# A recurrent-memory attention kernel with a gated unit: score matmuls set between projection matmuls, in place of a V stage with ten tile buffers and transposing DMAs

## The chip, the cores and the metric

The kernel runs on one core of a Trainium2 chip. The metric is device time in microseconds of one execution. The kernel before has a median of 1620.66 us over four runs (1619.23 to 1621.8). The profile below comes from one more execution, which took 1622.41 us; its span, from the first to the last instruction, is 1620.70 us, and the remaining 1.7 us lie around it.

## The reference, cut to what matters

A layer norm feeds two branches whose product is added to x:

```python
def _A_ref(x, mem0, Wq, Wk, Wv, Wo, seg_len):      # 32 heads of 128, segments of 32, memory of 8
    ...
    for s in range(n_seg):
        h = jnp.concatenate([mem, xs], axis=1)      # 8 memory + 32 token rows
        q, k, v = ...                               # h @ Wq, h @ Wk, h @ Wv
        p = _softmax(jnp.where(mask[None, None], scores, -1e9), axis=-1)
        o = jnp.einsum('bhte,hed->btd', jnp.einsum('bhqk,bhke->bhqe', p, v), Wo)
        mem = o[:, :M, :].copy()                    # memory of the next segment
        outs.append(o[:, M:, :])
def _B_ref(x, w_gate, w_up, w_down):
    h = _sigmoid(x @ w_gate) * (x @ w_up)
    return h @ w_down
x = A_x; xn = _layernorm(x)
return x + _A_ref(xn, ...) * _silu(_B_ref(xn, ...))
```

There are 2048 tokens of 1024 features, hence 64 segments, and the gated unit has 3584 hidden features.

## The kernel before, in words

The loop over segments is not run one by one. Memory rows are estimated in advance from sums of V over each segment, all segments then go through attention together, and a check at the end raises a flag if the estimate was not good enough (a sequential version stands behind that flag). Tokens are held as 16 tiles of 128; xnT is the normalized input with features on partitions, 8 chunks of 128 (KC = 8).

**The V stage** (lines 274 to 480) computes V for all tokens. Its unit is a pair (g, t): column group g of 1024 (of 4) for token tile t (of 16), in two halves of 512 columns (`v_half`, L354): eight matmuls each (L361) into a PSUM buffer of `psb` (four buffers, tag "big"), which ACT copies to the tile v_sb (L363). `v_store` (L365) sends v_sb to vp_dram from SP's queue; `seg_sums` (L375) adds up segments on DVE; `gather_sums` (L379) moves the sums in 16 small copies; `wo_part` (L402) multiplies them by a piece of Wo on TensorE. `normalize` (L311) makes one tile of the normalized input, and `transpose_x` (L327) turns it by eight PE transposes (L330) and an ACT copy (L332). `pack` (L340) copies xnT into xq, where memory rows are interleaved. Weights come by `load_wv` (L288) and `wo_load` (L397).

The order is a list written by hand, `units` (L424): tiles 0 to 7 for group 0, then for group 1, then tiles 8 to 15, each for group 0 and group 1, then groups 2 and 3. Tiles 8 to 15 are not turned on TensorE. `store_xn` (L334) writes them to xn_dram and `turn_xn` (L337) reads them back with a transposing DMA, both on SP's queue. V tiles come from `vs2`, ten buffers on the right side of the memory, until `begin_glu` (L254) closes that pool at unit 57 and opens the gate pools in its place; the last units use `vsp`, three buffers. Every half is copied by ACT. Within this stage TensorE, SP, ACT and DVE follow program order.

**Between V and the heads** (L481 to L541) the memory estimates are worked out, with steps of the gate and up matmuls (`glu_gate_up_steps`, L145; `filler`, L261) filling TensorE.

**The heads stage** (L544 to L672) runs 32 heads in a pipeline of one head's length. While head h is projected (`proj_steps`, L578: q and k, five blocks each, eight matmuls of 424 columns per block, L589, and an ACT copy at its end, L591), head h-1 does its attention (`attn_steps`, L641). Its scores come in five batches (`s_batch`, L594): matmuls of 99 columns (L603), one for the first segment (L605), then Exp on ACT (L607) and a mask on DVE (L609). P times V comes in seven groups of three matmuls and a single one (`pv_batch`, L613; L628, L623), each followed by a reciprocal and a product on DVE (L631, L632). A plan by hand sets which of them stand after which of the ten projection blocks:

```python
plan = [[("s", 0), ("s", 1)], [("s", 2)], [("s", 3)], [("s", 4), ("v", 0)], [("v", 1)], [("v", 2), ("v", 3)],
        [("v", 4)], [("v", 5), ("v", 6)], [("v", 7)], []]
```

So scores run back to back, nine at first and four or five afterwards, and PV three or six at a time. Here TensorE and SP follow program order. In the last turn of the loop no head is projected, and `filler` steps stand between the plan's steps.

**After the heads** the rest of the gate and up matmuls, then the down projection (L763), the output projection (L773) and the combination. The change touches none of that.

Of the kernel before, what the change touches and what calls it, by code (L numbers as in the profile page):

```python
# [19 lines left out]
P = 128  # L20
# [183 lines left out]
def kernel(ctx, tc, A_x, A_mem0, A_Wq, A_Wk, A_Wv, A_Wo, A_seg_len, B_x, B_w_gate, B_w_up, B_w_down, out,  # L204
# [34 lines left out]
    xn_dram = tc.dram_tile([S // 2, DM], BF16, name="xn_dram")  # L239
# [10 lines left out]
    es_r = ExitStack()  # L250
    vs2 = es_r.enter_context(tc.tile_pool(name="vs2", bufs=10, side="right"))
    glus = []

    def begin_glu():  # L254
        es_r.close()
        gu_w = es_x.enter_context(tc.tile_pool(name="gu_w", bufs=2, side="right", reuse_waits="tile"))
        gu_sb = es_x.enter_context(tc.tile_pool(name="gu_sb", bufs=2, side="right", reuse_waits="tile"))
        glus.append(glu_gate_up_steps(nc, gu_w, gu_sb, xnT, B_w_gate, B_w_up, hT_dram, psb, "big", 4))
        filler(1)

    def filler(n=1):  # L261
        for _ in range(n):
            next(glus[0], None)
# [10 lines left out]
    with ExitStack() as es:  # L274
# [31 lines left out]
        svqa = hwp.tile([P, 2, NT, 1024 // SEG], F32, name="svqa", tag="w")  # L306
        svqs = [svqa[:, 0], svqa[:, 1], svq, svq]
# [26 lines left out]
        def store_xn(t):  # L334
            nc.sync.dma_start(xn_dram[(t - NT // 2) * P:(t - NT // 2 + 1) * P, :], xns[t][:])

        def turn_xn(t):  # L337
            nc.sync.dma_start_transpose(xnT[:, :, t * P:(t + 1) * P], xn_dram[(t - NT // 2) * P:(t - NT // 2 + 1) * P, :])

# [14 lines left out]
        def v_half(g, t, j):  # L354
            if j == 0:
                v_sbs[g, t] = (vsp if glus else vs2).tile([P, 1024], BF16, name="v_sb")
            v_sb = v_sbs[g, t]
            cg = 2 * g + j
            v_ps = psb.tile([P, 512], F32, name="v_ps", tag="big")
            for c in range(KC):  # L360
                nc.tensor.matmul(v_ps[:], lhsT=xnT[:, c, t * P:(t + 1) * P], rhs=wv_sb[:, c, cg * 512:(cg + 1) * 512],  # L361
                                 start=(c == 0), stop=(c == KC - 1))
            nc.scalar.copy(v_sb[:, j * 512:(j + 1) * 512], v_ps[:])  # L363

        def v_store(g, t):  # L365
            v_sb = v_sbs[g, t]
# [8 lines left out]
        def seg_sums(g, t):  # L375
            nc.vector.tensor_reduce(svqs[g][:, t, :], v_sbs[g, t][:].rearrange("p (b i) -> p b i", i=SEG), axis=AX.X, op=ALU.add,
                                    apply_transpose=True)

        def gather_sums(g):  # L379
            src = svqs[g][:, :, :].rearrange("p t (h b) -> p b h t", b=4)  # L380
# [42 lines left out]
        HT = NT // 2  # L423
        units = [(g, t) for g in range(2) for t in range(HT)]  # L424
        units += [(g, t) for t in range(HT, NT) for g in range(2)]
        units += [(g, t) for g in range(2, NG) for t in range(NT)]
        turns = {HT + 2 * i: HT + i for i in range(4)}
        turns.update({2 * HT + 2 * i: HT + 4 + i for i in range(4)})
        loads = {2 + i: (2 + i // 2, i % 2) for i in range(4)}
        loads.update({18 + 3 * i: (4 + i // 2, i % 2) for i in range(4)})  # L430
        loads.update({38 + 2 * i: (6 + i // 2, i % 2) for i in range(4)})
        wload = {n: hg for hg, n in enumerate((33, 35, 39, 42, 50, 54, 59, 61))}
        wpart = (38, 41, 44, 47, 55, 58)
        for n, (g, t) in enumerate(units):
            if n == 0:
                v_half(0, 0, 0)
                transpose_x(1)
                normalize(2)
                v_half(0, 1, 0)
                normalize(3)  # L440
                for c in range(KC):
                    nc.tensor.transpose(mt0[:, c, :], m0[:, c * P:(c + 1) * P], ident[0:M, 0:M])
                nc.vector.tensor_copy(cmT[:, :, NM:NCM], mt0[:])
                nc.vector.tensor_copy(xq[:, :, X0 + SEG:NP], mt0[:])
                nc.vector.tensor_copy(g1b[:, :, NM:NCM], mt0[:])
                transpose_x(2)
                v_half(0, 0, 1)
            elif n == 1:
                v_half(0, 1, 1)
            else:  # L450
                v_half(g, t, 0)
                v_half(g, t, 1)
            v_store(g, t)
            if 0 < n < HT - 3:
                normalize(n + 3)
            if 0 < n < HT - 2:
                transpose_x(n + 2)
            if n in turns:
                normalize(turns[n])
                store_xn(turns[n])  # L460
            if n - 2 in turns:
                turn_xn(turns[n - 2])
            if n > 0:
                seg_sums(*units[n - 1])
            if g == 1:
                pack(t)
            for k, q in ((2 * NT, 0), (2 * NT, 1), (3 * NT, 2)):
                if n == k:
                    o1 = gather_sums(q)
                    pend += [(2 * q, o1, 0), (2 * q + 1, o1, 4)]  # L470
            if n in loads:
                cg, i = loads[n]
                load_wv(cg, i * 4, i * 4 + 4, nc.scalar)
            if n == 57:
                begin_glu()
            if n in wload:
                wo_ts.append(wo_load(wload[n], nc.scalar))
            if n in wpart:
                hg, o1, h0 = pend.pop(0)
                wo_part(acc1, wo_ts.pop(0), hg, o1[:, h0:h0 + 4, :])  # L480
        es_v.close()  # L481
        wo_t = wo_ts
        seg_sums(*units[-1])
# [65 lines left out]
    with ExitStack() as es:  # L549
# [28 lines left out]
        def proj_steps(h):  # L578
# [5 lines left out]
            for (w_, dst) in ((wq, qt), (wk, kt)):  # L584
                for i in range(NBLK):
# [5 lines left out]
                    nc.scalar.copy(dst[:, a:b], pr[:, 0:b - a])  # L591
                    yield

        def s_batch(h, i):  # L594
# [6 lines left out]
            for j in range(n):  # L601
                o = (j0 + j) * TR
                nc.tensor.matmul(s_ps[:, j * TR:(j + 1) * TR], lhsT=kt[:, o:o + P], rhs=qt[:, o:o + TR], start=True, stop=True)  # L603
            if last:
# [5 lines left out]
            if last:  # L610
                nc.vector.tensor_tensor(pT[0:L, X0:NP], pT[0:L, X0:NP], mask0[:], op=ALU.mult)

        def pv_batch(h, i):  # L613
# [10 lines left out]
            else:  # L624
                R = TR
                for j in range(n):
                    o = (j0 + j) * TR
                    nc.tensor.matmul(o_ps[:, j, :], lhsT=pT[:, o:o + P], rhs=va[:, j0 + j, v0:v0 + DH + 1],  # L628
                                     start=True, stop=True)
            rd = rden[0:R, h, j0:j0 + n]  # L630
            nc.vector.reciprocal(rd, o_ps[0:R, 0:n, d0])  # L631
            nc.vector.tensor_tensor(osb[0:R, j0:j0 + n, hh * DH:(hh + 1) * DH], o_ps[0:R, 0:n, e0:e0 + DH],  # L632
                                    rd.unsqueeze(2).to_broadcast([R, n, DH]), op=ALU.mult)

# [5 lines left out]

        def attn_steps(h):  # L641
            st["p", h] = pTs[h % 2]
            plan = [[("s", 0), ("s", 1)], [("s", 2)], [("s", 3)], [("s", 4), ("v", 0)], [("v", 1)], [("v", 2), ("v", 3)],
                    [("v", 4)], [("v", 5), ("v", 6)], [("v", 7)], []]
            for step in plan:
                for kind, i in step:
                    (s_batch if kind == "s" else pv_batch)(h, i)
# [3 lines left out]
        for h in range(H + 1):  # L651
            pj = proj_steps(h) if h < H else None
            at = attn_steps(h - 1) if h > 0 else None
            for i in range(2 * NBLK):
                if i == 4 and h % 2 == 1 and h + 1 < H:
# [201 lines left out]
```

## Time and profile before

| what | us |
|---|---|
| median of four runs | 1620.66 |
| lowest to highest | 1619.23 to 1621.8 |
| profiled execution | 1622.41 |
| its span | 1620.70 |
| TensorE busy | 1607.7 (99%) |
| VectorE busy | 525.2 (32%) |
| ScalarE busy | 408.9 (25%) |
| V stage, up to its last matmul | about 243 |
| heads stage | 323 to 852 |
| gate, up | 852 to 1193 |
| down, output | 1193 to 1620.7 |

Some of the costliest groups of the page:

```profile
L589 PE MATMUL pr<-xq,wqk 128*128 128x424 bf16 x2560 | 501.3, 342 | 0.0
...
L361 PE MATMUL v_ps<-wv_sb,xnT 128*128 128x512 bf16 x1024 | 224.2, 379 | 5.2 <-DMA xnT<-xn_dram 1.7
...
L363 ACT CAST v_sb<-v_ps 128x512 bf16<-128x512 f32 x128 | 74.5, 585 | 155.0 <-PE v_ps L361 141.3
```

How to read them: line, engine, operation, output <- inputs, shape, count, then busy time and the mean time of one in ns, then the idle time of the engine just ahead of them and what ended most of it. The mean of a matmul is its time from start to end; matmuls overlap, and the time that one adds to the queue is the distance between starts. A weight load (PEld) runs beside the matmul ahead of it.

### The profile page before, as it was taken

To read this page: it belongs to the slowest core of one execution; us is meant where nothing else is said; L and a number is where in the kernel's file an instruction comes from. 1 tells how busy PE (TensorE), PEld (TensorE's weight loads), DVE (VectorE), ACT (ScalarE), POOL (GpSimd) and SP (SyncE) were. 2 spreads that over 40 slices of the span, in tenths; PEclk is the share of its full clock that TensorE was granted. 3 is DMA by queue.
4 is the path that set the end of the run, shared out by engine and by line. 5 is a ranking of instruction groups with operands and counts; after the bars stand their busy time and mean duration, and the time that the engine had idled before them with its cause. 6 is when DMAs were issued, how large, how long until landed. Compare 5 with 4: busy or idle time off the path is not lost.

```text
span 1620.7 us, 24042 instructions
## 1 busy us (share of the span) xinstructions
PE 1607.7 (99%) x10135; PEld 837.0 (52%) x10135; DVE 525.2 (32%) x1224; ACT 408.9 (25%) x788; POOL 97.6 (6%) x145
## 2 busy tenths in 40 slices
PE   9999999999999999999999999999999999999998
PEld 4444445756666666666664444444454444444444
DVE  6655434324443444444443212221212111111111
ACT  4333321144444444444442111111100000000000
POOL 0000000001000010000001011111100000000000
PEclk9999999999999999999999999999999999999999
DMA  6795455543534343333413535352451433424350
GB/s 212 151 172 177 159 171 175 192 125 105 138 104 120 94 124 104 86 102 89 119 36 87 188 120 191 117 169 66 108 125 61 124 98 108 117 95 130 75 130 28
DMA packets 232124, 198.08 MB, mean 122 GB/s; under 512 B 85512, under 2 KB 189656, under 8 KB 231996
## 3 DMA queue, kind: packets, MB, share of 16 engines
q1 hardware_dynamic: 207564, 141.56, 32.9%
q0 software_dynamic: 13872, 40.23, 7.9%
q10 hardware_dynamic: 10576, 14.70, 2.8%
q8 instruction: 81, 1.33, 0.3%
q14 instruction: 31, 0.25, 0.0%
HBM read 112.80 MB, written 64.08 MB: 109 GB/s over the span
## 4 chain that ended last, share of the span: by engine, by line
PE 95%; DMA 4%; DVE 1%; ACT 0%; issue 0%; SPq 0%; ACTq 0%
PE pr L589 28%; PE a_ps L773 14%; PE y_ps L763 12%; PE u_ps L172 12%; PE g_ps L168 12%; PE v_ps L361 10%; PE o_ps L628 2%; PE s_ps L603 2%; DMA xnT<-xn_dram 1%; DMA wv_sb<-in_A_Wv_dram 1%; PE acc L405 1%; DMA vp_dram<-v_sb 1%; DMA xn_dram<-xn 1%; PE vm_ps L524 1%; PE vm_ps L500 1%; PE wo_ps L726 1%
## 5 line engine op out<-in xcount | busy, mean ns | idle before, releaser
L589 PE MATMUL pr<-xq,wqk 128*128 128x424 bf16 x2560 | 501.3, 342 | 0.0
L589 PEld LDWEIGHTS <-wqk 128*128 128x128 bf16 x2560 | 237.1, 97 | 166.1
L361 PE MATMUL v_ps<-wv_sb,xnT 128*128 128x512 bf16 x1024 | 224.2, 379 | 5.2 <-DMA xnT<-xn_dram 1.7
L773 PE MATMUL a_ps<-wo_sb,ot 128*128 128x512 bf16 (+1 forms) x1056 | 226.0, 373 | 0.0
L172 PE MATMUL u_ps<-xnT,wu 128*128 128x512 bf16 x896 | 211.7, 379 | 1.8 <-DVE hst L176 1.8
L168 PE MATMUL g_ps<-xnT,wg 128*128 128x512 bf16 x896 | 211.7, 379 | 0.1
L763 PE MATMUL y_ps<-wd,ht 128*128 128x512 bf16 x896 | 198.1, 379 | 0.0
L176 DVE SCALAR_TENSOR_TENSOR hst<-th,u_ps 128x512 bf16<-128x512 f32 x112 | 77.0, 688 | 295.1 <-PE u_ps L172 289.2
L773 PEld LDWEIGHTS <-ot 128*128 128x128 bf16 x1056 | 103.3, 98 | 118.0
L361 PEld LDWEIGHTS <-xnT 128*128 128x128 bf16 x1024 | 99.1, 98 | 124.1 <-DMA xnT<-xn_dram 3.8
L175 ACT ACTIVATE th<-g_ps 128x512 f32<-128x512 f32 x112 | 66.8, 597 | 328.2 <-PE g_ps L168 321.1
L172 PEld LDWEIGHTS <-wu 128*128 128x128 bf16 x896 | 87.7, 98 | 107.6 <-issue 2.0
L763 PEld LDWEIGHTS <-ht 128*128 128x128 bf16 x896 | 87.5, 98 | 105.0
L168 PEld LDWEIGHTS <-wg 128*128 128x128 bf16 x896 | 86.6, 98 | 101.6 <-issue 0.4
L591 ACT CAST kt<-pr 128x424 bf16<-128x424 f32 x160 | 81.9, 512 | 183.2 <-PE pr L589 145.2
L632 DVE TENSOR_TENSOR osb<-o_ps,rden 99x384 bf16<-99x384 f32 (+1 forms) x256 | 126.1, 513 | 4.4
L609 DVE TENSOR_TENSOR pT<-pT,mask 99x396 bf16<-99x396 bf16 (+1 forms) x160 | 59.6, 379 | 187.3 <-ACT pT L607 187.3
L766 ACT ACTIVATE th<-y_ps 128x512 f32<-128x512 f32 x32 | 19.1, 597 | 391.8 <-PE y_ps L763 391.8
L363 ACT CAST v_sb<-v_ps 128x512 bf16<-128x512 f32 x128 | 74.5, 585 | 155.0 <-PE v_ps L361 141.3
L591 ACT CAST qt<-pr 128x424 bf16<-128x424 f32 x160 | 81.9, 512 | 117.4 <-PE pr L589 117.4
L631 DVE RECIPROCAL rden<-o_ps 99x3 f32<-99x3 f32 (+1 forms) x256 | 44.8, 178 | 116.2 <-PE o_ps L628 103.6
L607 ACT ACTIVATE pT<-s_ps 99x396 bf16<-99x396 f32 (+2 forms) x160 | 81.2, 531 | 4.0 <-PE s_ps L603 2.6
(104 smaller groups left out, 694.6 us busy)
## 6 DMA issues: line engine op xcount, KB each, us to landing
va<-vp_dram SPq DMA_DIRECT2D x16, 1039.5 KB
o_dram<-osb POOLq DMA_DIRECT2D x16, 1039.5 KB, 12.3
vp_dram<-v_sb SPq DMA_DIRECT2D x60, 256.0 KB
hT_dram<-hst POOLq DMA_DIRECT2D x56, 256.0 KB, 3.0
ht<-hT_dram SPq DMA_DIRECT2D x16, 896.0 KB
xt<-in_A_x_dram SPq DMA_DIRECT2D x32, 256.0 KB
wo_t<-in_A_Wo_dram ACTq DMA_DIRECT2D x8, 1024.0 KB
wo_t<-in_A_Wo_dram SPq DMA_DIRECT2D x8, 1024.0 KB
```

The source lines that it names most:

```text
L168: nc.tensor.matmul(g_ps[:], lhsT=wg[:, c, fc * P:(fc + 1) * P], rhs=xnT[:, c, tb * TB:(tb + 1) * TB], start=(c == 0), stop=(c == KC - 1))
L172: nc.tensor.matmul(u_ps[:], lhsT=wu[:, c, fc * P:(fc + 1) * P], rhs=xnT[:, c, tb * TB:(tb + 1) * TB], start=(c == 0), stop=(c == KC - 1))
L175: nc.scalar.activation(th[:], g_ps[:], ACTF.Tanh, scale=0.5)
L176: nc.vector.scalar_tensor_tensor(hst[:, :, fc, :], th[:].rearrange("p (a b) -> p a b", b=P), 1.0, u_ps[:].rearrange("p (a b) -> p a b", b= ...
L361: nc.tensor.matmul(v_ps[:], lhsT=xnT[:, c, t * P:(t + 1) * P], rhs=wv_sb[:, c, cg * 512:(cg + 1) * 512], start=(c == 0), stop=(c == KC - 1))
L363: nc.scalar.copy(v_sb[:, j * 512:(j + 1) * 512], v_ps[:])
L589: nc.tensor.matmul(pr[:, 0:b - a], lhsT=w_[:, c, hc], rhs=xq[:, c, a:b], start=(c == 0), stop=(c == KC - 1))
L591: nc.scalar.copy(dst[:, a:b], pr[:, 0:b - a])
L607: nc.scalar.activation(pT[0:TR, o:o + w], s_ps[0:TR, 0:w], ACTF.Exp, scale=scale)
L632: nc.vector.tensor_tensor(osb[0:R, j0:j0 + n, hh * DH:(hh + 1) * DH], o_ps[0:R, 0:n, e0:e0 + DH], rd.unsqueeze(2).to_broadcast([R, n, DH]) ...
L763: nc.tensor.matmul(y_ps[:], lhsT=hts[t][:, c, :], rhs=wd[:, c, hf * 512:(hf + 1) * 512], start=(c == 0), stop=(c == FC - 1))
L773: nc.tensor.matmul(a_ps[:], lhsT=ox[t][0][:, h, :], rhs=wo_sb[:, h, a:b], start=(h == 0), stop=(h == H - 1))
```

## The change

It puts two things in the place of two others.

The V stage gets one plain order: group by group, and in each group all 16 tiles. All 16 tiles are turned by `transpose_x`; xn_dram, `store_xn`, `turn_xn`, `vs2`, `svqa` and `begin_glu` are gone, and the gate pools stand from the start. All V tiles come from `vsp` with three buffers. The second half of a tile is copied by DVE in groups 1 to 3. `gather_sums` runs once at the first unit of groups 1, 2 and 3. Loads of Wv for the next group stand at tiles 6, 8, 10 and 12, of Wo at tiles 1 and 5 of groups 1 to 3 and at 11 and 13 of the last, and the first gate weights at tile 4 of the last.

In the heads, every generator gives way after each matmul. One turn of the loop is one projection matmul (80 a head), and after every second one a single score matmul of the former head follows, from slot 0 to slot 42. From the third block on, behind the block's first projection (slots 16, 24, ... 72), one PV group of three follows. Exp, mask, reciprocal and product stay with the last matmul of their batch or group.

```diff
-    es_r = ExitStack()
-    vs2 = es_r.enter_context(tc.tile_pool(name="vs2", bufs=10, side="right"))
...
+    gu_w = es_x.enter_context(tc.tile_pool(name="gu_w", bufs=2, side="right"))
+    gu_sb = es_x.enter_context(tc.tile_pool(name="gu_sb", bufs=2, side="right"))
+    glu = glu_gate_up_steps(nc, gu_w, gu_sb, xnT, B_w_gate, B_w_up, hT_dram, psb, "big", 4)
...
-        def store_xn(t):
-            nc.sync.dma_start(xn_dram[(t - NT // 2) * P:(t - NT // 2 + 1) * P, :], xns[t][:])
-
-        def turn_xn(t):
-            nc.sync.dma_start_transpose(xnT[:, :, t * P:(t + 1) * P], xn_dram[(t - NT // 2) * P:(t - NT // 2 + 1) * P, :])
...
-                v_sbs[g, t] = (vsp if glus else vs2).tile([P, 1024], BF16, name="v_sb")
+                v_sbs[t] = vsp.tile([P, 1024], BF16, name="v_sb")
...
-            nc.scalar.copy(v_sb[:, j * 512:(j + 1) * 512], v_ps[:])
+            if j == 0 or g == 0:
+                nc.scalar.copy(v_sb[:, j * 512:(j + 1) * 512], v_ps[:])
+            else:
+                nc.vector.tensor_copy(v_sb[:, j * 512:(j + 1) * 512], v_ps[:])
...
-        for n, (g, t) in enumerate(units):
...
+        for g in range(NG):
+            for t in range(NT):
...
+                v_store(g, t)
+                if g == 0 and 0 < t < NT - 3:
+                    normalize(t + 3)
+                if g == 0 and 0 < t < NT - 2:
+                    transpose_x(t + 2)
+                if g == 0 and t > 0:
+                    seg_sums(t - 1)
+                if g == 1:
+                    pack(t)
+                if g > 0 and t == 0:
+                    seg_sums(NT - 1)
+                    o1 = gather_sums(g - 1)
+                    pend += [(2 * (g - 1), o1, 0), (2 * (g - 1) + 1, o1, 4)]
+                elif g > 0:
+                    seg_sums(t - 1)
+                if g < NG - 1 and t in (6, 8, 10, 12):
+                    i = (t - 6) // 2
+                    load_wv(2 * g + 2 + i // 2, i % 2 * 4, i % 2 * 4 + 4, nc.scalar)
+                if g == NG - 1 and t == 4:
+                    filler(1)
+                if g == NG - 1 and t in (11, 13):
+                    wo_ts.append(wo_load(6 + (t == 13), nc.scalar))
+                if pend and t in (1, 5):
+                    wo_ts.append(wo_load(pend[len(wo_ts)][0], nc.scalar))
+                if pend and t in (6, 10):
+                    hg, o1, h0 = pend.pop(0)
+                    wo_part(acc1, wo_ts.pop(0), hg, o1[:, h0:h0 + 4, :])
...
                         nc.tensor.matmul(pr[:, 0:b - a], lhsT=w_[:, c, hc], rhs=xq[:, c, a:b],
                                          start=(c == 0), stop=(c == KC - 1))
-                    nc.scalar.copy(dst[:, a:b], pr[:, 0:b - a])
-                    yield
-
-        def s_batch(h, i):
+                        if c == KC - 1:
+                            nc.scalar.copy(dst[:, a:b], pr[:, 0:b - a])
+                        yield
+
+        def s_steps(h, i):
...
                 nc.tensor.matmul(s_ps[:, j * TR:(j + 1) * TR], lhsT=kt[:, o:o + P], rhs=qt[:, o:o + TR], start=True, stop=True)
+                if last or j < n - 1:
+                    yield
...
-        def pv_batch(h, i):
+            yield
+
+        def pv_steps(h, i):
...
+                    if j < n - 1:
+                        yield
...
+        NSL = 2 * NBLK * KC
+
         def attn_steps(h):
             st["p", h] = pTs[h % 2]
-            plan = [[("s", 0), ("s", 1)], [("s", 2)], [("s", 3)], [("s", 4), ("v", 0)], [("v", 1)], [("v", 2), ("v", 3)],
-                    [("v", 4)], [("v", 5), ("v", 6)], [("v", 7)], []]
-            for step in plan:
-                for kind, i in step:
-                    (s_batch if kind == "s" else pv_batch)(h, i)
+            ss = (x for i in range(len(sbat)) for x in s_steps(h, i))
+            vv = (x for i in range(len(pbat)) for x in pv_steps(h, i))
+            for k in range(NSL):
+                if k % 2 == 0:
+                    next(ss, None)
+                if k % KC == 0 and k >= 2 * KC:
+                    for _ in range(3):
+                        next(vv, None)
                 yield
...
-            for i in range(2 * NBLK):
-                if i == 4 and h % 2 == 1 and h + 1 < H:
+            for i in range(NSL):
+                if i == 4 * KC and h % 2 == 1 and h + 1 < H:
...
-                if pj is None:
+                if pj is None and i % KC == KC - 1:
                     filler(1)
```

## The prediction, made before the change was run

> **What bounds the kernel now.** I read the page first: share of busy time, the 40 slices, the chain.
>
> ```profile
> PE 1607.7 (99%) x10135; PEld 837.0 (52%) x10135; DVE 525.2 (32%) x1224; ACT 408.9 (25%) x788; POOL 97.6 (6%) x145
> ...
> PEclk9999999999999999999999999999999999999999
> ...
> PE 95%; DMA 4%; DVE 1%; ACT 0%; issue 0%; SPq 0%; ACTq 0%
> ```
>
> TensorE is the path everywhere, at full granted clock. A change can only pay by taking matmuls, or the small gaps between them, off that engine. Both halves of this change do so in different stages, so I next asked for busy time by stage.
>
> ```profile
> 17.80:243.20 225.40, 222.02 (x1220) 104.15 (x1218) 118.30 (x188) 78.28 (x140) 0.00 (x0) 1.00 0.66 168
> 243.20:323.00 79.80, 77.78 (x1086) 50.84 (x1085) 28.64 (x76) 13.77 (x25) 6.18 (x8) 1.00 0.57 185
> 323.00:852.00 529.00, 528.89 (x3926) 320.06 (x3927) 220.20 (x699) 229.14 (x474) 31.58 (x30) 1.00 0.38 103
> ```
>
> The columns are stretch, length, then busy time of PE, PEld, DVE, ACT, POOL. The V stage (first row) leaves PE a few us idle, the start of the gate stage (second) two more, the heads (third) nothing: there only matmul spacing counts. The chain within the V stage and the timeline after it say what the idle time waits for.
>
> ```profile
> 33.62 10.49 DMA wv_sb<-in_A_Wv_dram
> ...
> 79.06 11.26 DMA xnT<-xn_dram
> ...
> 110.64 9.65 DMA xnT<-xn_dram
> ...
> 233.82 12.52 DMA vp_dram<-v_sb
> ```
>
> ```profile
> 246.44 1.07 ACT L363 CAST v_sb<-v_ps 128x512 bf16<-128x512 f32 x2 [3.98 <-DMA vp_dram<-v_sb]
> ...
> 248.82 4.57 DVE L384 COPY svT<-svq 32x128 f32<-32x128 f32 x16
> ...
> 253.43 0.69 DVE L176 SCALAR_TENSOR_TENSOR hst<-th,u_ps 128x512 bf16<-128x512 f32 x1
> 254.17 1.89 PE L172 MATMUL u_ps<-xnT,wu 128*128 128x512 bf16 x8 [1.75 <-DVE hst L176]
> ```
>
> The last V cast waits 4 us for a store to free its tile. That delays the sums, the 16 copies and the first gate product, and PE stands. From single start times in the trace, less the 215.8 ns at which 512-column matmuls follow each other, the waits are: 1.24 us at 42.7 (Wv not landed); 0.46, 0.78, 1.55 at 89.7, 104.0, 118.6 (the transposing DMA); 0.25 and 1.92 at 246.6 and 252.0. Together 6.2 us.
>
> **V stage, removed.** The transposing DMAs go, with their 2.79 us. The Wv wait goes too: group 1 is now needed only at unit 16, some 55 us after its first load may start. The eight xn stores and eight transposes leave SP's queue, where one issue took 2.5 to 4.5 us; no x load or V store waits behind them any more. Nothing else is late in those places, as tiles 2 to 7 show: normalize, transpose by PE, two halves, every 3.90 us with no gap (units at 17.82, 21.71, 25.61).
>
> **V stage, added.** 64 PE transposes, eight per tile. The row is one unit with and one without: 3.90 against 3.45 us, so 0.448 us a tile, 8 tiles = **+3.58 us**, all on the path. Their evictions are 8 ACT copies of 1.0 us; ACT then has 0.59 x 2 + 1.0 + 0.3 = 2.5 of 3.9 us, as in tiles 2 to 7: hidden. The Trainium skill (TensorE: Matmul & The Clock Gate, Part 4) speaks against this step: a PE transpose is given as about 275 ns in a kernel's context, which by it would make +17.6 us. The record here also reads 219 ns, but eight start within 0.45 us, so the measured 56 ns apiece decides.
>
> **The second half's cast on DVE** for groups 1 to 3 (48 casts). No such row is in the trace; the nearest are a 280-column PSUM copy at 450 ns and the 512-column hst at 688, so 0.45 to 0.69; I take 0.67. DVE then has 0.67 + 1.24 (sums) + 0.39 (pack) = 2.3 of 3.45 us: hidden. At each group's first unit it also gathers, 4.57 + 0.43 us, with the next cast queued behind. In group 1 cast, pack, sums, gather and cast end 8.3 us after the unit's last matmul; PE wants that PSUM buffer (four of them) after 3.45 + 5.18 = 8.6. Zero, with 0.3 us to spare.
>
> **Three V tiles in place of ten.** A tile is refilled 3 x 3.45 = 10.4 us after its first cast, and its store is issued 2.3 us after that cast. So a landing within 8.0 us costs nothing, and the four PSUM buffers let casts run another 4.1 us late (3 halves of 1.73 less a cast and its start). Landing events in the trace give 6.2 to 8.7 us for stores alone or beside one Wo load, 8.6 to 12.5 between 134 and 180, where four 1 MB Wo and four 512 KB Wv loads fall into 16 units. Now 16 units hold two Wo and four Wv loads, spread, so I expect 6 to 10. Low end: no stall. High end: eight units in each of groups 1 and 2 at the 10.6 mean of that busy stretch. A held tile casts both halves at once, so its cycle is 1.5 + 10.6 = 12.1 us against 10.4, 0.58 us lost per unit, 9.3 us in all, less 2 x 4.1 slack = 1. Gate weights beside two Wo loads in group 3 may add 2 to 4. Behind a held cast on ACT stand the next casts and Wv's load issues, on DVE the sums; PE only feels it through the PSUM buffers. I take 0.6, with 0 and 5 as ends: it is nearer to the quiet rows.
>
> **Start of the gate stage.** The gate weights load at unit 52 in place of 57, so the last stores should land near 8 us, not 12.5; the last sums end some 4.0 us after V's end, not 5.65. Copies 4.57 and hst 0.69 later is 9.3; PE wants that buffer at 8.6. So 0.4 (0 to 1.9) is left of 2.17.
>
> V stage and gate start: 3.58 + 0.6 + 0.4 - 6.2 = **-1.6 us** (-2.6 to +4.3).
>
> **Heads: scores one by one.** Which row prices them?
>
> ```profile
> 408.98 0.35 PE L603 MATMUL s_ps<-qt,kt 128*128 128x99 bf16 x4
> 409.16 1.60 PE L589 MATMUL pr<-xq,wqk 128*128 128x424 bf16 x8
> ```
>
> Four scores take 182 ns of the queue. Start to start over 30 heads, a score in the middle of a run takes 47.4 ns, the first after a projection 44.1 (44 to 45), the last before a projection 44.5; a projection takes 178.9 in a run, 179.2 before a score, 178.5 after one. Placed singly, all 21 are first and last at once: 21 x 44.1 + 30 (the 40-column one) = 956 ns a head against 1003 now, x 32 = -1.5 us; no gain at all if the single one keeps 47.4 (+0.1). I take the first-after-a-projection row, which has both neighbours' kinds in it.
>
> **PV in threes** changes from six runs a head to eight. A PV after a projection takes 60.9 against 56.6 ns, one after a score 55.8; a projection after PV 182.5 against 178.9. Now: 5 entries x 4.3 + 6 exits x 3.5 = 43 ns. Then: four groups follow a score, four a projection: 17 + 8 x 3.5 = 45; if all eight pay, 62. So +0.1 to +0.6 us, I take +0.2. Heads: **-1.3 us** (-1.4 to +0.7).
>
> **Cover that could go.** PV group 0 now stands at slot 16. Counted from the start of block 0's last projection (slot 7) it comes after ten projections and five scores: 10 x 179 + 5 x 44 = 2.01 us. Block 0's cast starts 0.38 after that origin, Exp 0.41 later, the mask 0.62 after that (rows at 406 us) and takes 0.42: 1.83, plus a signal. Cover: under 0.15 us, where before it was whole blocks. Behind the waiting weight load stands TensorE's whole queue, so whatever is missing is paid in full. Each later group has 0.17 more, the PV before it.
>
> **Sum.** -1.6 - 1.3 = -2.9 us. The profiled execution took 1622.41 us with span 1620.70; it would become 1619.5. The median of the runs shown is 1620.66, 1.75 below that execution: **1617.8 us**. A measurement of this kernel tells about 0.2%, 3.2 us, from no change, so the forecast lies just inside "same" (1617.4 to 1623.9).
>
> **Rivals.** (1) *Three tiles bind.* For: ACT already waits 12.7 us in five casts for stores, in the only units that share three tiles. Against: PE lost only 0.25 us directly by it. Stalls of 3 to 7 us: 1619.8 to 1623.8, just over at worst. Chance 0.13. (2) *Group 0 waits for its mask*, 0.1 to 0.2 us in 31 heads: +3.1 to +6.2 on the forecast, 1620.9 to 1624.0. Chance 0.08. (3) *The change does not do what it says:* single scores keep 47.4 ns, heads +0.3: 1619.4. Chance 0.05. (4) *Slower: the weight load after a single score is laid open.* Each score must now cover a projection's load in 44 ns, 704 times; the load's record reads 98 ns. Fully open it is 54 x 704 = 38 us, 1656; it decides against the change from 9 ns each. Against it: the last score of a run is already followed by a projection after 43 to 47 ns. Chance 0.08. The Trainium skill's section on LDWEIGHTS (same page) gives 128 columns / 1.2 = 107 ns per load, +44 us by it; the spacing of runs in this trace denies it.
>
> **Chances.** Forecast 0.66, its own range 1616.4 to 1619.6 (-4.0 us, and 0.3 for the spread of the median, to 1.8 us more stall than taken): 0.30 of it below 1617.4, 0.36 within. Rival 1: 0.09 same, 0.04 slower; rival 2: 0.06 and 0.02; rival 3: 0.05 same; rival 4: 0.08 slower. Faster 0.30, same 0.56, slower 0.14. The range 1616.4 to 1624.0 takes in the bounds of the buffer cost and leaves out rival 4 and the far ends.
>
> **What would show it.** Right: no DMA wait of PE before 240 us; v_ps units of 3.90 us up to tile 13; ACT's or DVE's waits on V stores, but PE gaps there under 1.5 us; last u_ps wait well under 1.75; s_ps rows with 44 ns spacing; 32 heads 1.3 us shorter. Wrong: a PE wait on the ACT or DVE cast in groups 1 to 3 repeated each third unit, o_ps L628 waiting for DVE pT, or projections that start over 50 ns after a score.

## The result and the profile after

| | before | after |
|---|---|---|
| median, us | 1621.6 (60 runs, 1618.97 to 1626.07) | 1619.61 (40 runs, 1618.53 to 1620.5) |
| ratio | | 0.9987, 95% interval 0.9983 to 0.9992 |
| profiled execution, us | 1622.41 | 1618.69 |
| its span, us | 1620.70 | 1617.0 |

The change makes the kernel 0.13% faster, about 2.1 us (1.3 to 2.8), inside the 0.2% that the prediction called "same". The forecast of 1617.8 us is 1.8 us low: the result lies within the whole range (1616.4 to 1624.0) and at the upper end of the forecast's own (1619.6). Of this, 0.9 us lies in the starting figure (1620.66 over four runs, 1621.6 over sixty), and 0.9 in the change itself, forecast at -2.9 us.

The page of the kernel after, its share of busy time, its chain, and the three groups that the prediction names:

```profile
PE 1608.2 (99%) x10199; PEld 839.2 (52%) x10199; DVE 563.4 (35%) x1272; ACT 392.5 (24%) x748; POOL 97.6 (6%) x145
...
PE 97%; DMA 2%; DVE 1%; ACT 0%; issue 0%; DVEq 0%; SPq 0%; ACTq 0%
...
L565 PE MATMUL pr<-xq,wqk 128*128 128x424 bf16 x2560 | 520.7, 342 | 0.0
...
L345 PE MATMUL v_ps<-wv_sb,xnT 128*128 128x512 bf16 x1024 | 224.8, 379 | 1.7 <-ACT xnT L322 1.4
...
L580 PE MATMUL s_ps<-qt,kt 128*128 128x99 bf16 x672 | 137.6, 208 | 0.0
```

TensorE is still the path. It has 64 instructions more (the transposes) and the DMA share of the chain fell from 4% to 2%. One trap stands in the line of pr: its busy time is 19 us above that of before (501.3), and yet the heads are shorter. Matmuls overlap, so the busy time of a group depends on how other matmuls cut it up. Only the distance between starts tells what one costs the queue.

By stage, same columns as in the prediction:

```profile
17.20:242.50 225.30, 224.95 (x1282) 107.84 (x1280) 146.76 (x234) 58.39 (x101) 0.00 (x0) 1.00 0.46 151
242.50:320.40 77.90, 77.61 (x1089) 51.01 (x1088) 30.15 (x77) 13.39 (x24) 6.18 (x8) 1.00 0.59 187
320.40:848.70 528.30, 528.30 (x3929) 318.91 (x3928) 228.45 (x698) 232.64 (x474) 31.58 (x30) 1.00 0.38 103
```

PE's idle time fell from 3.4 to 0.35 us in the V stage and from 2.0 to 0.3 in the gate's start. From start to start in the two traces: from V's last matmul to the first projection 80.18 became 78.02 us (-2.16), from the first to the last projection 528.90 became 528.02 (-0.88), and V ended 0.68 us sooner, all of it ahead of the transposes of tile 2 (13.46 became 12.76 us), where this execution waited less for its first loads. The rest of the kernel, 423.14 us from the last gate or up matmul to the last output matmul, is the same.

The V stage, in the chain of waits of the kernel after (start, length, what):

```profile
24.63 0.45 PE pt L320 x8
25.08 3.45 PE v_ps L345 x16
...
196.31 6.45 DMA vp_dram<-v_sb
...
203.64 16.38 DMA vp_dram<-v_sb x2
...
221.04 3.61 PE v_ps L345 x16
```

The first two lines are the price of a turned tile, 0.45 + 3.45 us, now up to tile 15. The others are three stores in a row that the casts waited for: three tiles do bind, in one place.

The start of the gate stage in the kernel after (start, length, engine, line; in brackets the idle time before and who ended it):

```profile
245.89 1.71 DVE L371 COPY svT<-svq 32x128 f32<-32x128 f32 x6
247.63 0.69 DVE L176 SCALAR_TENSOR_TENSOR hst<-th,u_ps 128x512 bf16<-128x512 f32 x1
248.35 2.88 DVE L371 COPY svT<-svq 32x128 f32<-32x128 f32 x10
...
251.32 1.89 PE L172 MATMUL u_ps<-xnT,wu 128*128 128x512 bf16 x8
```

There is no bracket on PE's lines: the wait of 1.92 us is gone. But look at DVE: the first gate product (hst) does not follow the 16 copies, it stands after the sixth. DVE's order after the V stage is left to the planner (the tool that orders instructions where the program does not), and the planner chose another one. Nobody wrote that in the change.

### The profile page after: what moved, and what is told of

Its sections match the earlier page's. It is cut to its first block, busy times and chain, and to the rows that moved or that the text cites. A ratio compares the mean times of both kernels' runs of the same rounds, so it can differ in the third digit from the quotient of the medians.

```text
span 1617.0 us, 24231 instructions
## 1 busy us (share of the span) xinstructions
PE 1608.2 (99%) x10199; PEld 839.2 (52%) x10199; DVE 563.4 (35%) x1272; ACT 392.5 (24%) x748; POOL 97.6 (6%) x145
## 4 chain that ended last, share of the span: by engine, by line
PE 97%; DMA 2%; DVE 1%; ACT 0%; issue 0%; DVEq 0%; SPq 0%; ACTq 0%
PE pr L565 28%; PE a_ps L761 14%; PE y_ps L751 12%; PE g_ps L168 12%; PE u_ps L172 12%; PE v_ps L345 12%; PE o_ps L608 2%; PE s_ps L580 2%; DMA vp_dram<-v_sb 1%; PE acc L392 1%; PE vm_ps L500 1%; PE vm_ps L476 1%; PE wo_ps L714 1%; PE pt L320 0%; DVE svT L371 0%; DMA xt<-in_A_x_dram 0%
## 5 line engine op out<-in xcount | busy, mean ns | idle before, releaser
L565 PE MATMUL pr<-xq,wqk 128*128 128x424 bf16 x2560 | 520.7, 342 | 0.0
L565 PEld LDWEIGHTS <-wqk 128*128 128x128 bf16 x2560 | 209.2, 97 | 125.6
L580 PE MATMUL s_ps<-qt,kt 128*128 128x99 bf16 x672 | 137.6, 208 | 0.0
L614 DVE TENSOR_TENSOR osb<-o_ps,rden 99x384 bf16<-99x384 f32 (+1 forms) x256 | 134.0, 523 | 8.8
L580 PEld LDWEIGHTS <-kt 128*128 128x128 bf16 x672 | 65.2, 98 | 54.2
```

Of the source, the lines that this page charges most:

```text
L565: nc.tensor.matmul(pr[:, 0:b - a], lhsT=w_[:, c, hc], rhs=xq[:, c, a:b], start=(c == 0), stop=(c == KC - 1))
```

## The experiments

Times are compared with runs of the kernel before on the same chip. The ratios and their intervals are those on record; they can differ by some 0.0004 from the quotient of the two medians beside them. "Stage" numbers are from start to start in the trace of one execution.

### The heads alone, and V alone

The two halves of the change, each put into the kernel before: in the first only `proj_steps` to the loop over heads is new, in the second only the V stage.

```diff
 # heads alone, in the kernel before
-        def s_batch(h, i):
+        def s_steps(h, i):
...
-            for i in range(2 * NBLK):
+            for i in range(NSL):
 # V alone, in the kernel after
-        def s_steps(h, i):
+        def s_batch(h, i):
...
-            for i in range(NSL):
+            for i in range(2 * NBLK):
```

> The kernel before with the new heads alone; its V stage, ten V tiles and transposing DMAs stay. Theory (the heads gain little, the rest of the gain is PE's idle time before 260 us): 0.9 us less, as the two profiles' heads differ (528.9 to 528.0 us), ratio 0.9994; PE's waits on xnT before 120 us stay at 2 to 4 us. Rival (the heads are the whole gain, and the profiled waits of the V stage are those of one execution): about 2 us less, ratio 0.9987.

> The changed kernel with the heads of before: scores in runs, PV by the old plan. Theory: 64 transposes cost 3.6 us, the waits on transposing DMAs, Wv and the first gate product (6.2 us in the profile of before) go, 0.5 us comes back for three tiles: 1.1 to 2.1 us less, ratio 0.9987 to 0.9993. Rival (the heads are the whole gain): the same time as before, ratio 1.0000.

Heads alone took 1620.78 us (11 runs) beside 1621.26 (1617.67 to 1624.22, 33 runs) for before, ratio 0.9994 (0.9985 to 1.0003). V alone took 1620.24, 0.9997 (0.9988 to 1.0006). Neither time tells the halves apart; the stages do. With the heads alone, the heads take 528.02 us and the rest is as before (80.59 from V's end to the first projection, beside 80.18). With V alone, the heads take 528.90 and that stretch 78.01. So the gains are separate and add up: -0.88 and -2.16.

The V stage settles the third term. Counted from tile 2's transposes to the last V matmul, the five executions with the former V stage (before, heads alone, and three runs further below: hst first and the two with rounded addresses) take 229.69, 228.69, 230.58, 229.30 and 228.84 us. Less PE's waits for transfers in each (4.03, 3.04, 4.91, 3.66 and 3.19) this is 225.64 to 225.68. The new V stage without a stall takes 229.21 in four traces (two with three tiles, two with four). The 64 transposes thus cost +3.55 us. The waits that went with the old order differ from run to run, 3.0 to 4.9 us: the exchange is nearly even.

### Why the wait at the gate's start went

Two readings: the last stores landed earlier, as I had predicted, or DVE's order changed. One experiment delays the gate weights in the kernel after. The other changes only the order in the kernel before: `es_v.close()` ends the stretch in which ACT and DVE keep program order, and it is moved down past four lines.

```diff
 # gate weights late (kernel after)
-                if g == NG - 1 and t == 4:
+                if g == NG - 1 and t == 9:
 # hst first (kernel before)
-        es_v.close()
         wo_t = wo_ts
         seg_sums(*units[-1])
         filler(1)
         o1 = gather_sums(NG - 1)
+        es_v.close()
```

> The changed kernel with the first gate weights asked for at tile 9 of the last group in place of tile 4 (unit 57, as before). Theory (the last sums were late because the last V stores landed late, and those because gate weights and Wo loads fell among them): the last V stores land 10 us or more after issue, the last cast waits 3 to 4 us, and PE waits again 1 to 2 us for the first gate product near 250 us. Rival (the wait went because DVE now takes the first gate product among the 16 copies and not behind them): no PE wait there.

> The kernel before, with one order changed: on DVE the first gate product (hst) stands ahead of the 16 small copies of the last segment sums, where the kernel before has it behind them. Theory (the wait of 1.92 us that PE had at the start of the gate stage came from that order, and not from how late the last V stores land): the last sums still end near 248.8 us, hst then ends near 249.5, PE wants its buffer near 252.2, so the wait is 0; from V's last matmul to the first projection 80.2 becomes 78.3 us, ratio to before 0.9988. Rival (the late stores are the cause, and the wait only moves): the copies now end 0.7 us later, and either the gate's next PSUM buffer or the Wo product that needs the sums is late by 0.7 us or more; the stretch stays at 79.5 us or longer.

With late gate weights (1620.3 us, one run) the three stores issued from 226 to 234 us land 10.9 to 12.7 us later, and the last casts wait for stores:

```profile
244.84 0.58 ACT L348 CAST v_sb<-v_ps 128x512 bf16<-128x512 f32 x1 [2.95 <-DMA vp_dram<-v_sb]
...
247.86 1.71 DVE L371 COPY svT<-svq 32x128 f32<-32x128 f32 x6
...
249.60 0.69 DVE L176 SCALAR_TENSOR_TENSOR hst<-th,u_ps 128x512 bf16<-128x512 f32 x1
...
251.83 1.89 PE L172 MATMUL u_ps<-xnT,wu 128*128 128x512 bf16 x8
```

Counted from V's end the copies start 1.5 us later than in the kernel after, and PE still does not wait: the stretch is 78.18 us. Now the former order and the new one in the former V stage. Heads alone, where DVE has the former order:

```profile
245.57 1.07 ACT L363 CAST v_sb<-v_ps 128x512 bf16<-128x512 f32 x2 [4.25 <-DMA vp_dram<-v_sb]
...
247.95 4.58 DVE L384 COPY svT<-svq 32x128 f32<-32x128 f32 x16
252.56 0.69 DVE L176 SCALAR_TENSOR_TENSOR hst<-th,u_ps 128x512 bf16<-128x512 f32 x1
...
253.30 1.89 PE L172 MATMUL u_ps<-xnT,wu 128*128 128x512 bf16 x8 [1.76 <-DVE hst L176]
```

and the kernel before with hst first:

```profile
247.30 1.07 ACT L363 CAST v_sb<-v_ps 128x512 bf16<-128x512 f32 x2 [3.97 <-DMA vp_dram<-v_sb]
...
250.31 0.69 DVE L176 SCALAR_TENSOR_TENSOR hst<-th,u_ps 128x512 bf16<-128x512 f32 x1 [0.66 <-ACT th L175]
250.92 4.58 DVE L384 COPY svT<-svq 32x128 f32<-32x128 f32 x16
...
253.27 1.89 PE L172 MATMUL u_ps<-xnT,wu 128*128 128x512 bf16 x8
```

The cast waits 4 us for its store in both. Only the place of hst differs, and PE's bracket is gone: 78.01 us, the kernel after's own figure, from one moved line. The time is 1620.16 (10 runs) beside 1621.21 (1619.69 to 1622.86, 21 runs), ratio 0.9991 (0.9982 to 1.0). The rival's new wait did not come. Order alone is enough. Earlier stores with the former order were not tried, but the lines of the kernel after allow an estimate. From the first copy to the end of hst the former order takes 5.3 us (247.95 to 253.25 with the heads alone). The kernel after starts its copies at 245.89, so hst would have ended there near 251.2, and PE took the buffer at 251.32. In a second execution of the same kernel the copies start at 246.30 and PE takes the buffer at 251.02: hst would have been 0.6 us late. So the earlier stores alone would have left 0 to 0.6 of the 1.9 us, by this estimate; each cause goes most of the way by itself.

### What a V tile buffer is worth

```diff
-tc.tile_pool(name="vs", bufs=3)
+tc.tile_pool(name="vs", bufs=4)
-name="o1", tag="o1", bufs=2)
+name="o1", tag="o1", bufs=1)
```

The second pair makes the room. The other run has `bufs=2` for the pool vs and nothing else.

> The changed kernel with four V tiles in place of three (room for it comes from o1, one buffer in place of two). Theory (three tiles cost TensorE only the one gap of 0.5 us at 220 us, though ACT and DVE wait 124 us for stores): that gap goes, ACT's and DVE's waits on vp_dram fall below 40 us, and the time is 0.5 us less than the changed kernel's, at most 1.0. Rival (three tiles bind, differently in each execution): 1.5 us or more less than the changed kernel.

> The changed kernel with two V tiles in place of three. Theory (a tile is free only when its store has landed, 6 to 9 us after its issue, and only the number of tiles hides that): with two, a tile is wanted again 6.9 us after its first cast, and its cycle is a cast of 0.7, a wait for the issue of some 0.5 and a landing of 6 to 9 us, so 3.6 to 5.1 us a unit in place of 3.45: 10 to 100 us longer in the V stage, with PE's waits put down to the casts of ACT and DVE, and theirs to vp_dram. Rival (landings are long only because three or more stores are under way at once): with two, landings fall to 5 us and the V stage is at most 5 us longer.

Four tiles: 1618.86 us (11 runs, 1618.49 to 1619.37), ratio to before 0.9985 (0.9976 to 0.9994). What the casts waited for stores, in the kernel after:

```profile
ACT v_sb L348 <- DMA vp_dram<-v_sb: 95.4, 30, 7.1
...
DVE v_sb L350 <- DMA vp_dram<-v_sb: 28.7, 18, 4.5
...
PE v_ps L345 <- ACT v_sb L348: 0.3, 1, 0.3
```

and with four tiles:

```profile
ACT v_sb L348 <- DMA vp_dram<-v_sb: 6.1, 2, 4.2
```

(The columns are total us, times, longest.) Of 124 us of waiting by ACT and DVE, PE felt one gap of 0.51 us. The rest lies in the slack of four PSUM buffers and costs nothing, so taking it away gains 0.5 us.

Two tiles: 1652.16 us (one run). From tile 2's transposes to V's end 261.26 us, +32.05. The stores land 6.8 us after their issue in the median, nearly all between 5.5 and 10; with three tiles the median is 8.0. Fewer stores under way do land somewhat sooner, so the rival's mechanism is there in part, but not at its 5 us, and the stage is 32 us longer where the rival allowed 5. The longest of the waits (SP's queue, then ACT and PE): the store of 233.11 us was issued right behind the gate weights and landed 12.9 us later.

```profile
230.24 1.76 SPq L155 DMA_DIRECT2D wu<-in_B_w_up_dram  x1
233.11 16.75 SPq L360 DMA_DIRECT2D vp_dram<-v_sb  x4
...
246.06 0.59 ACT L348 CAST v_sb<-v_ps 128x512 bf16<-128x512 f32 x1 [8.53 <-DMA vp_dram<-v_sb]
...
246.70 3.57 PE L345 MATMUL v_ps<-wv_sb,xnT 128*128 128x512 bf16 x8 [5.48 <-ACT v_sb L348]
```

Not all of the 32 us are waits: the clock fell to half after three of the gaps (last section), for 11.5 us of matmuls, which cost some 5.8. Three buffers stand just at the edge: one less costs 32 us, one more saves the 0 to 0.9 us for which PE stands in six traces with three.

### Fewer, longer PV runs, and PV without a switch of rows

In the first, PV comes in four runs of six instead of eight of three. In the second, P and V tiles have 128 partitions (the added rows zero), so that PV uses 128 active rows like the projections.

```diff
 # PV in sixes
-                if k % KC == 0 and k >= 2 * KC:
-                    for _ in range(3):
+                if k % KC == 0 and k // KC in (3, 5, 7, 9):
+                    for _ in range(6):
 # PV over 128 rows
-        vas = [vp.tile([TR, NTL + 1, VW], BF16, name=f"va{i}") for i in range(2)]
+        vas = [vp.tile([P, NTL + 1, VW], BF16, name=f"va{i}") for i in range(2)]
...
+            nc.vector.memset(va[96:P, 0:NTL, :], 0.0)
...
-        pTs = [vp.tile([TR, NPA], BF16, name=f"pT{i}") for i in range(2)]
+        pTs = [vp.tile([P, NPA], BF16, name=f"pT{i}") for i in range(2)]
...
+            nc.vector.memset(pT[96:P, 0:NP], 0.0)
```

> The changed kernel with PV groups set two at a time at blocks 3, 5, 7 and 9 (four entries a head in place of eight). Theory (each entry into PV costs 4.3 ns and each way back to projections 3.6 ns, whatever stands around it): 4 x 7.9 ns x 32 = 1.0 us less than the changed kernel; the third matmul after an entry keeps 56 ns. Rival (the ways in and out are hidden, or the second group waits for its PSUM buffer): the same, or longer, with o_ps waits on DVE.

> The changed kernel with P and V kept on 128 partitions, the 29 added ones zero, so that PV's matmuls use 128 rows like all others. Theory (TensorE pays about 4 ns to go from 128 rows to 99 and 3.6 ns back): the first PV falls from 60.8 to 56 ns, the projection behind PV from 182.5 to 178.9; 8 x 7.9 x 32 = 2.0 us less than the changed kernel in the heads. Rival (the 4 ns belong to a change of PSUM bank or operand, not of rows): the same spacing and time.

PV in sixes: 1620.23 us, 0.9994 (0.9985 to 1.0003); the heads take 527.56, that is -0.46 us against the kernel after, half of what I expected. The ways in and out that went were paid back in part: inside a run a PV now takes 56.5 ns where threes have 55.9, and a projection 179.0 where it had 178.8.

128 rows: 1620.5 us (11 runs) beside 1621.93 (1619.09 to 1623.35, 15 runs), 0.9995 (0.9986 to 1.0004). The cost of changing over goes: a PV first after a projection takes 56.6 ns in place of 60.9, a projection after PV 178.9 in place of 182.5. But PV inside a run rises from 55.9 to 58.0, a projection inside a run from 178.8 to 179.1. The heads take 528.70, with one new stall of 1.56 us in the first head; without it 527.14, -0.88 where I expected -2.0. The stall:

```profile
338.62 0.51 ACT L570 CAST qt<-pr 128x424 bf16<-128x424 f32 x1 [1.10 <-PE pr L567]
339.02 0.98 ACT L588 ACTIVATE pT<-s_ps 99x495 bf16<-99x495 f32 x2
339.72 0.70 DVE L590 TENSOR_TENSOR pT<-pT,mask 99x495 bf16<-99x495 bf16 x2 [6.16 <-ACT pT L588]
...
340.20 0.34 PE L610 MATMUL o_ps<-va,pT 128*128 128x129 bf16 x3 [1.40 <-DVE pT L590]
```

The planner put the first Exp behind the cast of the second block, and PV group 0 has no cover for that.

### Four tiles and 128 rows together

The edits of the two runs together, with the zeros written by POOL (against the 128-row run):

```diff
-            nc.vector.memset(va[96:P, 0:NTL, :], 0.0)
+            nc.gpsimd.memset(va[96:P, 0:NTL, :], 0.0)
-            nc.vector.memset(pT[96:P, 0:NP], 0.0)
+            nc.gpsimd.memset(pT[96:P, 0:NP], 0.0)
```

> The changed kernel with four V tiles in place of three (one buffer less for the gathered sums makes the room) and PV over 128 active rows in place of 99, so that PE does not switch its active rows between projections and PV; the zeros for the added rows are written by POOL, where an earlier run of mine wrote them on DVE and the first head then stood 1.56 us. Theory (both gains are additive, the stall came from DVE's late start): V without its 0.5 us gap, from the first to the last projection 527.1 us in place of 528.0; 1.4 us less than the changed kernel, near 1618.3, ratio to before 0.9978. Rival (POOL's memsets take 2 to 5 us each and hold up the loads of the first head's V): a stall of 1 to 4 us stays in the first head, and the sum is 0 or a loss of up to 3 us against the changed kernel.

1620.77 us (11 runs, 1617.64 to 1624.49), 0.9995 (0.9986 to 1.0004): no gain over the kernel after. The V gap is gone (229.21 us), the spacings are those of the 128-row run, but the first head is worse. The rival held. The first head in this run:

```profile
325.77 9.16 POOL L533 MEMSET va<- 32x5418 bf16 x2 [12.21 <-DVE va L534]
...
330.76 0.30 SPq L551 DMA_DIRECT2D va<-vp_dram  x1
...
331.10 4.98 SPq L552 DMA_DIRECT2D va<-vp_dram  x1
...
342.75 0.48 PE L610 MATMUL o_ps<-va,pT 128*128 128x129 bf16 x3 [2.74 <-DMA va<-vp_dram]
```

The memset of one V tile takes 4.6 us on POOL against 2.32 on DVE, where the same zeros are written as 32x2709 words of four bytes. That width is the difference: the zeros of a P tile, 32x2119 bf16 on both, take 1.86 us on POOL and 1.82 on DVE, and all four rows come to 0.85 to 0.88 ns for each element in a partition. V's load for the first head is issued behind it, at 330.76 us where the kernel after has it at 321.96, and the first PV waits for that load. And the heads (531.48 us) are 4.3 us longer than 527.14 though the gap in PE's starts is only 2.9. The clock in these microseconds (stretch, PE busy, granted clock):

```profile
343.00:344.00 1.00, 1.00 (x7) 0.50 0.43 113
...
345.00:346.00 1.00, 1.00 (x7) 0.62 0.84 184
346.00:347.00 1.00, 1.00 (x12) 1.00 0.84 165
```

PE starts again at 342.75, and until 345.75 TensorE runs at half its clock: another 1.4 us.

### Why a score inside a run takes 47.4 ns and a single one 44

A guess was that the operands of neighbouring scores start at odd addresses. In these two runs, on the kernel before, the addresses of one operand are rounded down.

```diff
 # first
-rhs=qt[:, o:o + TR]
+rhs=qt[:, o // 16 * 16:o // 16 * 16 + TR]
 # second
-lhsT=kt[:, o:o + P]
+lhsT=kt[:, o // 16 * 16:o // 16 * 16 + P]
```

> The kernel before, with scores in runs, whose moving operand is read from a column rounded down to a multiple of 16 (so the scores are of other tokens: part of the computation is changed). Theory (inside a run a score takes 47.4 ns and not 44 because its moving columns start at odd addresses, 198 bytes apart; behind a long projection that is hidden): runs fall to about 44 ns, 1.3 us less in the heads. Rival (the weight load sets the 47.4): no change.

> The kernel before, with scores in runs, whose weights are loaded from a column rounded down to a multiple of 16 (the scores are of other tokens: part of the computation is changed). Theory (the moving operand's address sets the 47.4 ns): no change of spacing. Rival (the weight load from odd addresses sets it): about 44 ns, 1.3 us less in the heads.

Inside runs the scores took 46.7 and 47.3 ns, and the heads 528.54 and 528.85 us (528.90 before). The second took 1621.21 us. The first took 8831.65, because its scores made the kernel go through its sequential version too; only its heads are read. The moving operand's address explains at most 0.7 of 3.3 ns, that of the weights nothing. The cause of the 47.4 stays open; that a single score takes 44.0 is shown.

### The kernel after once more

> The changed kernel once more, as it is, for what differs between two executions of the same code. Theory (the small waits for transfers differ from run to run, the spacing of matmuls does not): from the first to the last projection 528.0 us and the spacings of scores and PV the same to 0.1 ns; the start-up, the V stage and the wait on the Wo product near 1210 us (0 in the first profile of this kernel, 0.5 to 1.4 in those of its relatives) differ by up to 1 us each. Rival (the spacing itself differs): the heads move by 0.3 us or more, and my reading of them holds only to that.

1618.63 us (one run). The heads take 528.02 us again, with the same spacings to 0.1 ns. V takes 229.22 from tile 2, where the first trace had 229.71 and the gap, and the tail 423.38 in place of 423.14. In the traces of its relatives a wait on the product with Wo near 1210 us is 0 to 1.4 us. So the spacing is a property of the code, while some 0.5 us in V and 1 us after the gate are the run's.

## Why the prediction was right, and where it missed

| step | predicted, us | measured, us |
|---|---|---|
| 64 transposes | +3.58 | +3.55 |
| waits for Wv and the transposing DMA | -4.03 | -3.0 to -4.9, mean -3.8 of five traces |
| three tiles | +0.6 (0 to 5) | 0 to 0.9, mean 0.4 of six traces |
| gate start | -1.8 | -2.16 |
| scores | -1.5 | -1.60 (46.34 to 44.06 ns x 672, and the 40-column one 29.6 to 27.5 x 32) |
| PV, with the way in and the way out | +0.2 (0.1 to 0.6) | +0.50 (PV 57.56 to 57.93 x 704: +0.26; the projection behind PV, eight a head in place of six: +0.24) |
| the other projections | 0 | +0.19 (all 2560 rose from 179.20 to 179.37, +0.43, less the 0.24) |
| sum | -2.9 | -2.0 by the medians, -1.3 to -2.8 by the ratio |

**V.** The transposes cost what the row said, 56 ns apiece also for the later tiles. The 275 ns of the Trainium skill (TensorE: Matmul & The Clock Gate, Part 4) is not what one of eight in a row costs here, and the granted clock stays at 1.0 through them. DVE's cast takes 0.69 us, 0.67 had been taken. The three tiles bind (124 us of waits on ACT and DVE) and PE hardly notices, as the reckoning with the PSUM slack had it. My term of -4.03 came from one execution and is a draw of that run; that V as a whole came out near the forecast (3.58 + 0.6 - 4.03, against 3.55 + 0.4 - 3.8 by the means) is in part luck.

**Gate start.** The size was nearly right, and the reason was one of two. The step "the last stores should land near 8 us, not 12.5" was to leave 0.4 of the wait. The last four land 7.1 to 9.3 us after issue, the sums end 3.4 us after V's last matmul starts (4.1 in the second execution; 4.0 had been taken), and by the estimate above this alone would have left 0 to 0.6. What I had not seen is DVE's order, which I took as fixed: with late stores and the new order there is no wait, and with the former V stage and the new order there is none either.

**Heads.** "21 x 44.1" held. Two terms were mis-sized. "Four groups follow a score" at 55.8 ns: the first PV after a score takes 60.8, like that after a projection, so all eight entries pay. The 55.8 had been read behind the 40-column score, the only one ahead of a PV in the kernel before. And I left the projections around a score alone: after a single score a projection takes 179.5 ns, where after a run of scores it took 178.5 and inside a run 178.9. Together the neighbours gave back 0.7 of the 1.6 us, where the prediction had 0.2. One slip in the sum stayed without effect: a single score that kept 47.4 ns would have cost (47.4 - 46.34) x 672 = +0.7 us, not the +0.1 of the prediction.

**Group 0.** The cover of under 0.15 us was right. Timeline of the kernel after, one head:

```profile
402.99 0.51 ACT L568 CAST qt<-pr 128x424 bf16<-128x424 f32 x1 [1.10 <-PE pr L565]
...
403.40 0.59 ACT L586 ACTIVATE pT<-s_ps 99x495 bf16<-99x495 f32 x1
...
404.02 0.42 DVE L588 TENSOR_TENSOR pT<-pT,mask 99x495 bf16<-99x495 bf16 x1 [3.48 <-ACT pT L586]
...
404.57 0.34 PE L608 MATMUL o_ps<-va,pT 99*128 99x129 bf16 x3
```

The mask ends at 404.44 and PV starts at 404.57, without a bracket; in 30 heads the distance is 0.12 to 0.13 us. In the 128-row run, where PE did wait, PV started 0.06 us after the mask, so no more than 0.07 us is to spare. Rival 2 missed by that much, and the 128-row run, in which the first Exp came one cast later, shows what it would have cost: 1.56 us for one head. Rival 4 is out: a projection starts 44 ns after a single score. Rival 3 is out by the same number.

**What stays open.** The stages of the traces add up to -3.1 us by their means (V +0.15, gate -2.36, heads -0.88; the former kernel's gate stretch is 80.18 to 80.59 us in four traces), and the timed runs say -2.0, with -2.8 as the near end of their interval. The differences between runs (start-up, V's transfers, the wait near 1210 us) are as large as the rest. The wait near 1210 us is 0.5 us in the mean of nine traces with the new V stage and 0.2 of five with the former one, which is the right way and too little; the traces are too few to settle it.

The best of the kernels here is the one with four tiles, 0.9985 to before; its interval overlaps that of the kernel after (0.9983 to 0.9992), so no gain over it is shown.

## What to carry to other kernels

Where one engine is full, price an instruction by the distance between starts with the neighbours that it will have, and price the neighbours again too: PV and the projections gave back 0.7 of the 1.6 us that the scores saved. A wait at a stage's border may hang on where a planner puts one short instruction; look at the order on that engine before crediting an earlier transfer alone, and try the order by itself, which here took 2.2 us off that stretch of the trace for one moved line (its timed ratio, 0.9982 to 1.0, does not show it by itself). A wait time summed over a helping engine (124 us) says nothing about the path; the slack behind it does.

## What the runs showed of the hardware

**A short stall costs more than its length.** Where 2.8, 2.9, 3.0 and 5.9 us lay between two starts (in the two-tile run, and in the run with four tiles and 128 rows) the granted clock fell to 0.50, and PE's matmuls ran so for 3.0 to 4.8 us; a 512-column matmul then started every 427 ns instead of 216. Where 1.6 to 2.1 us lay between them it stayed at 1.0. The fall can come late: behind the gap of 3.0 us, which ended at 178.45, matmuls kept 216 ns for another 1.3 us. From the two-tile run (stretch, its length, PE busy, granted clock); the first row is behind a gap of 2.1 us, the others behind 3.0 and 5.9:

```profile
162.00:164.00 2.00, 1.95 (x10) 1.00 0.25 53
...
178.00:180.00 2.00, 1.55 (x7) 0.94 0.20 74
180.00:183.00 3.00, 3.00 (x8) 0.50 0.46 105
...
247.00:250.00 3.00, 3.00 (x8) 0.50 0.22 44
```

The Trainium skill (TensorE: Matmul & The Clock Gate, HAM oscillation) gives about 3.4 us of idle time as the point to stay below; here 2.4 (2.78 less the 0.38 of the matmul before) was already too long in one case.

**Changing the number of active rows** between matmuls of 128 and 99 rows costs some 4 ns on the way in and 4 on the way out (60.9 against 56.6 ns, 182.5 against 178.9). It goes with 128 rows throughout, but then a PV in a run takes 2.1 ns more. Behind the 40-column score of the kernel before, the way in cost nothing (55.8 ns); why is open.
